# Hard-swish block's second product by Strassen, with its weights prepared on the chip and partly reloaded, and an earlier query transpose

## The chip, the cores and the metric

The kernel runs on one core of a Trainium2 chip. The metric is the device time of one execution in microseconds (us); the kernel before takes 975.52 us, the median of three runs (975.43 to 976.23). TensorE (PE) multiplies, ScalarE (ACT), VectorE (DVE) and GpSimd (POOL) work on elements, and SyncE (SP) issues the DMAs here. PEld is the loading of the stationary operand into TensorE, which overlaps the multiplying.

## The reference

Three stages follow each other. Chunked attention over 4 batches, 8 heads, 768 tokens of 64 (chunks of 32 with 16 keys to the left, 8 to the right, and 8 memory keys) gives x with 3072 tokens of 512. A first block of width 1024 with a gated softmax and a layer norm gives x2, again 3072 by 512. The third stage is the one that changes:

```python
def _moe2_ref(x, w_in, w_out):      # x: 3072 x 512, w_in: 512 x 2048, w_out: 2048 x 512
    h = x @ w_in
    relu6 = np.clip(h + 3.0, 0.0, 6.0)
    g = h * relu6 / 6.0
    return (g @ w_out).astype(np.float32)
```

Weights come as 64-bit floats, and the products are taken to float32 accuracy: each operand is split into a high and a low part of type fp32r, and a product is three matmuls, high by high, high by low and low by high.

## The kernel before

Tokens lie in 24 tiles of 128. A written-out list (FIRST) starts the pipeline, then a loop over tiles m = 7 to 23 runs the attention of the tiles ahead, the first product of block one for tile m (m1), its layer norm, and pieces of its second product (m2, called through piece) for groups of three tiles. Everything is issued in program order on each engine: there is no scheduler, so an engine's queue is the order of the calls, and a tile name (tag) that is used again makes the new writer wait for the last reader of the old content.

Inside a tile, block_p and block_e transpose the keys, p_p and p_e (line 467) the attention weights, v_p (line 476) multiplies them with the values, and q_p (line 410) transposes the queries of a later tile; v_p stands ahead of q_p. The third stage's weights are converted from 64 bits during the same loop (w2_abs, w2_hold, w2_bits), stored to DRAM as float32 (w2_store, w2d) and read back later (load_w2f, split_w2). The result x2 of block one goes through DRAM as well (m2_s, x2d, load_x2).

The third stage is a loop of 128 steps: 8 groups of 384 tokens by 16 slices of 128 of the inner width. In a step, g3 (line 649) makes 12 matmuls with a weight as the stationary operand and 384 token columns as the moving one. ACT and DVE then form the hard-swish r and split it into gh and gl. g4 (line 665) multiplies two steps later: for each of three token tiles, 3 matmuls with a 128 by 128 block of g stationary and 512 weight columns moving, 9 in all. Each matmul loads its stationary operand anew. All 32 weight slices lie split in SBUF from the first group on, so that in this stage only x2 is loaded and the output stored. The order of TensorE is g3 of step n, then g4 of step n-2:

```python
832         steps = [(gi, f) for gi in range(NG) for f in range(NF2)]
836                 g3(gi, f)
848                 g4(*steps[n - 2])
```

The functions that the diff touches, and what calls them:

## Time and profile before

| what | value |
|---|---|
| median of 3 runs | 975.52 us |
| the profiled execution | 976.84 us |
| its span in the profile | 975.1 us |
| PE busy | 947.0 us (97%) |
| weight loads (PEld) busy | 840.1 us (86%) |
| DVE / ACT / POOL busy | 53% / 42% / 16% |
| mean DMA rate over the span | 88 GB/s |
| granted TensorE clock | 0.997 of full speed |

A busy PE means that some matmul was in flight; since matmuls are pipelined, a row's duration is longer than the distance from one start to the next, and only that distance, or the time of a whole block of matmuls in the chain of waits, says what a matmul costs in a stream. Bounds between stages are read from the starts of the first and last matmul of a line.

### The profile page before, as it was taken

What the parts mean: (1) busy time and instruction counts of PE and PEld (TensorE: products, weight loads), DVE (VectorE), ACT (ScalarE), POOL (GpSimd) and SP (SyncE); (2) the same over time, 40 slices, a digit from 0 to 9 for tenths busy, and PEclk for the clock granted to TensorE, in tenths of its full rate; (3) what the DMA queues carried; (4) which work ended last, traced back from release to release, by engine and by line L of the source; (5) the groups of instructions that cost most, each with busy time, mean ns of one, the idle gap of its engine ahead of it and who ended that gap; (6) DMA issues with size and microseconds to landing.
All of it is one profiled execution on the core that took longest, in us unless ns stands there. A gap on an engine that the chain in (4) does not pass through costs nothing.

```text
span 975.1 us, 15592 instructions
## 1 busy us (share of the span) xinstructions
PE 947.0 (97%) x6108; PEld 840.1 (86%) x6108; DVE 517.7 (53%) x925; ACT 408.1 (42%) x730; POOL 154.6 (16%) x123
## 2 busy tenths in 40 slices
PE   5899899999999999999999999999999999999998
PEld 4677698888888888999999999999999999999997
DVE  6899977787878786446532232322322322323222
ACT  2568645656565654326432232332322322323322
POOL 3637742333332320000000000000000000000000
PEclk9999999999999999999999999999999999999999
DMA  9898156766766663144310010010010100100000
GB/s 179 162 215 193 53 146 192 170 165 188 180 174 179 166 163 93 66 132 134 118 41 25 1 66 1 1 65 1 1 65 1 59 6 1 66 1 1 33 1 32
DMA packets 129524, 86.16 MB, mean 88 GB/s; under 512 B 102828, under 2 KB 115116, under 8 KB 129452
## 3 DMA queue, kind: packets, MB, share of 16 engines
...
q8 instruction: 48, 0.79, 0.4%
...
## 4 chain that ended last, share of the span: by engine, by line
PE 77%; DVE 8%; issue 7%; DMA 4%; ACT 2%; POOL 1%; SPq 1%; DVEq 0%; POOLq 0%; ACTq 0%
PE ph L655 28%; PE acc L676 27%; PE m L599 9%; PE h L514 7%; PE tp L483 2%; PE sc L427 2%; DMA kn<-in_k_dram 1%; DVE lst L523 1%; PE tp L571 1%; DVE w2t L229 1%; DMA q_raw<-in_q_dram 1%; PE tp L414 1%; ACT pb L209 1%; DVE so L564 1%; DVE w2t L232 1%
## 5 line engine op out<-in xcount | busy, mean ns | idle before, releaser
L676 PE MATMUL acc<-w,gh 128*128 128x512 f32 x768 | 238.8, 392 | 0.0
L659 DVE SCALAR_TENSOR_TENSOR r<-r,ph 128x384 f32<-128x384 f32 x128 | 70.9, 554 | 278.4 <-ACT r L658 278.4
L658 ACT ACTIVATE r<-ph,three 128x384 f32<-128x384 f32 x128 | 74.4, 582 | 284.8 <-PE ph L655 284.8
L676 PEld LDWEIGHTS acc<-w,gh 128*128 128x128 f32 x768 | 142.3, 188 | 22.7
L676 PE MATMUL acc<-w,gl 128*128 128x512 f32 x384 | 151.1, 394 | 0.0
L655 PE MATMUL ph<-x,w 128*128 128x384 f32 x768 | 144.5, 336 | 0.0
L655 PE MATMUL ph<-x2h,w 128*128 128x384 f32 x512 | 141.0, 337 | 0.0
L655 PEld LDWEIGHTS ph<-x,w 128*128 128x128 f32 x768 | 136.0, 188 | 5.4
L237 DVE TENSOR_TENSOR gl<-r,gh 128x384 fp32r<-128x384 f32 x128 | 71.5, 558 | 75.7 <-ACT gh L236 75.7
L236 ACT ACTIVATE gh<-r 128x384 fp32r<-128x384 f32 x128 | 67.2, 525 | 80.0 <-DVE r L659 80.0
L655 PEld LDWEIGHTS ph<-x2h,w 128*128 128x128 f32 x512 | 93.7, 188 | 2.5
L599 PE MATMUL m<-lnh,wol 128*128 128x384 f32 x256 | 88.6, 346 | 1.5 <-POOL wol L327 0.9
L599 PE MATMUL m<-lnh,woh 128*128 128x384 f32 x256 | 88.2, 344 | 1.1 <-ACT woh L209 0.5
L599 PE MATMUL m<-lnl,woh 128*128 128x384 f32 x256 | 88.4, 345 | 0.3 <-DVE lnl L252 0.3
L655 PE MATMUL ph<-x2l,w 128*128 128x384 f32 x256 | 86.1, 336 | 0.0
L676 PEld LDWEIGHTS acc<-w,gl 128*128 128x128 f32 x384 | 72.0, 188 | 16.0
L514 PE MATMUL h<-w1h,xh 128*128 128x512 f32 x168 | 71.1, 423 | 0.0
L514 PE MATMUL h<-w1h,xl 128*128 128x512 f32 x168 | 67.1, 400 | 1.2 <-DVE xl L252 1.2
L514 PE MATMUL h<-w1l,xh 128*128 128x512 f32 x168 | 66.8, 398 | 0.0
L222 POOL TENSOR_SCALAR w2t<-w2t 128x512 f32<-128x512 f32 x32 | 63.0, 1983 | 8.7 <-ACT w2t L215 8.7
L248 ACT ACTIVATE lnh<-tp 128x512 fp32r<-128x512 f32 x41 | 24.3, 598 | 65.8 <-PE tp L571 65.8
L599 PEld LDWEIGHTS m<-lnh,wol 128*128 128x128 f32 x256 | 48.6, 190 | 2.4 <-POOL wol L327 1.2
...
## 6 DMA issues: line engine op xcount, KB each, us to landing
...
```

What stands on the lines that cost most here:

```text
L222: ENG[eng].tensor_scalar(out=tf, in0=tf, scalar1=U_LO, scalar2=U_HI, op0=ALU.max, op1=ALU.min)
L236: ACT.activation(out=hi, in_=r, func=AF.Copy)
L237: (eng or DVE).tensor_tensor(lo, r, hi.bitcast(F32), ALU.subtract)
L248: ACT.activation(out=hi, in_=r, func=AF.Copy)
L427: PE.matmul(sc[64 * x:64 * x + 64, c, s], qb[:, p, c].rearrange("k y t -> k (y t)"), kT[i % 2][:, p, c], start=True, stop=True)
L483: PE.matmul(po[64 * x:64 * x + 64, y, :, c * C:(c + 1) * C], vt[:, c, j], pb[:, c, j].rearrange("k s t -> k (s t)"), start=True, stop=True,)
L514: PE.matmul(h[:, f], a[:, kt], w[kt][:, f * 512:(f + 1) * 512], start=n == 0, stop=n == 3 * NKT - 1)
L599: PE.matmul(acc, w[fc // 2][:, fc % 2, dc * P:(dc + 1) * P], a[:, fc], start=n == 0, stop=n == len(todo) - 1)
L655: PE.matmul(ph, w[:, dc * P:(dc + 1) * P], xg[gi][a][:, dc], start=j == 0, stop=j == len(todo) - 1)
L658: ACT.activation(out=r, in_=ph, func=AF.Relu, bias=three, scale=1.0)
L659: DVE.scalar_tensor_tensor(out=r, in0=r, scalar=6.0, in1=ph, op0=ALU.min, op1=ALU.mult)
L676: PE.matmul(acc_t[t], a[:, sl], w, start=f == 0 and n == 0, stop=f == NF2 - 1 and n == 2)
```

## The change

The second product of the third stage, g @ w_out, is computed by Strassen's scheme: tokens are taken in 12 groups of 256 (two tiles) and the inner width in 8 pairs of slices, so that a step has a 2 by 2 grid of g blocks (128 by 128) and a 2 by 2 grid of weight blocks (128 by 256). Seven products of sums of blocks replace eight products of blocks. Of a step's 45 matmuls, all with 256 moving columns, 24 are of the first product and 21 (seven products, three each) of the second; there are 96 steps. POOL forms five sums of g blocks (one into q, four into s); ACT and DVE split two plain blocks with the sum in q, and then the four sums in s (split3). The seven products accumulate over the 8 pairs in four PSUM banks; at a group's end g_out copies three of them (ACT) and g_end combines them (six DVE operations, then two additions on POOL, or on DVE in the last group).

The five sums of weight blocks of each pair are formed by POOL during the tile loop (load_pair, sum_pair) and go to DRAM; prep splits them, and the two plain blocks, into seven high and low parts. SBUF holds six such sets at a time, and the pairs 1, 4 and 7 (USERS) share the tiles lh1 and km: their split sets are stored to DRAM once (store_prep) and read back by load_b, seven DMAs of 256 KB, each time after another user's products: 33 times in all. The weights of the first product (load_wi, split_wi) stay in SBUF. w1 of the first block moves to two larger tiles (wb0, wb1), which later hold prepared weights. In the tile loop the query transpose and its copies stand ahead of v_p for tiles of index 10 and above, and the last layer norm's transposes (ln_t) stand between the pieces of m2.

```diff
-    x2d = [dp.tile([P, NKT, G1], F32, name=f"x2d{i}") for i in range(NG)]
-    w2d = [dp.tile([P, 2, 512], F32, name=f"w2d{i}") for i in range(NF2)]
+    x2d = dp.tile([P, NKT, NT], F32, name="x2d")
+    w2d = [[dp.tile([P, 2, 512], F32, name=f"w2d{i}_{j}") for j in range(NF2 // 2)] for i in range(2)]
...
-        SP.dma_start(out=w2d[f][:, part], in_=raw["w2t", u].bitcast(F32))
+        SP.dma_start(out=w2d[part][f // 2][:, f % 2], in_=raw["w2t", u].bitcast(F32))
 
...
+    TG = 2 * P
+    NB = NT // TG
+    NS = NF2 // 2
+    USERS = (1, 4, 7)
+    B5_HOME = ("lh0", "lh1", "wb0", "wb1", "lh1", "ll1", "ll0", "lh1")
+    B2_HOME = (("kn0", "kn1"), ("km",), ("s0",), ("kT",), ("km",), ("q0", "q1"), ("s1",),
+               ("km",))
...
+    def load_pair(j):
+        raw["pair"] = T("xal", [P, 2, 2, 256], name="pair")
+        SP.dma_start(out=raw["pair"], in_=w2d[1][j].rearrange("p f (h c) -> p f h c", h=2))
+
+    def sum_pair(j):
+        w = raw["pair"]
+        t = raw["sums"] = T("x2r", [P, 5, 256], name="sums")
+        POOL.tensor_tensor(t[:, 0:2], w[:, :, 0], w[:, :, 1], ALU.add)
+        POOL.tensor_tensor(t[:, 2], w[:, 0, 0], w[:, 1, 1], ALU.add)
+        POOL.tensor_tensor(t[:, 3], w[:, 0, 1], w[:, 1, 1], ALU.subtract)
+        POOL.tensor_tensor(t[:, 4], w[:, 1, 0], w[:, 0, 0], ALU.subtract)
...
+    def prep():
+        j = PREPS[prep_n[1]]
+        prep_n[1] += 1
+        parts, d = raw["prep", j]
+        b5[j] = big(B5_HOME[j])[0]
...
+            split(t, b5[j][:, sl, 0], b5[j][:, sl, 1])
+        for k in range(2):
+            split(d[:, k], b2[j][k][:, 0], b2[j][k][:, 1])
+        load_prep()
+        store_prep()
+        to_store.append(j)
+
...
+    def load_b(j):
+        for u in (2, 3, 4, 1, 0):
+            SP.dma_start(out=b5[j][:, u].bitcast(F32), in_=b5_d[j][:, u])
+        for n in (1, 0):
+            SP.dma_start(out=b2[j][n].bitcast(F32), in_=b2_d[j][:, n])
...
-    def g3(gi, f):
-        n = gi * NF2 + f
-        ph = pp.tile([P, 512], F32, tag=("tp0", "tp1", "tp2", "sc")[n % 4], name="ph")[:, 0:G1]
-        wh, wl = w2h[f][:, 0], w2l[f][:, 0]
-        todo = [(dc, w, a) for dc in range(NKT) for w, a in ((wh, 0), (wh, 1), (wl, 0))]
-        for j, (dc, w, a) in enumerate(todo):
-            PE.matmul(ph, w[:, dc * P:(dc + 1) * P], xg[gi][a][:, dc],
-                      start=j == 0, stop=j == len(todo) - 1)
+    def g3(gi, j):
+        n = gi * NS + j
+        ph = pp.tile([P, 2, TG], F32, tag=("tp0", "tp1", "tp2", "sc")[n % 4], name="ph")
+        for k in range(2):
+            w = w2i[2 * j + k]
+            todo = [(dc, wl, xl) for dc in range(NKT) for wl, xl in ((0, 0), (0, 1), (1, 0))]
+            for m, (dc, wl, xl) in enumerate(todo):
+                PE.matmul(ph[:, k], w[:, wl, dc * P:(dc + 1) * P], xg[gi][xl][dc],
+                          start=m == 0, stop=m == len(todo) - 1)
+        ph_t[n] = ph.rearrange("p f t -> p (f t)")
...
+    def act3(gi, j):
+        n = gi * NS + j
+        rt = home(("pn", "pe")[n % 2], 896, F32)
+        r = rt[:, 0:512]
         ACT.activation(out=r, in_=ph, func=AF.Relu, bias=three, scale=1.0)
         DVE.scalar_tensor_tensor(out=r, in0=r, scalar=6.0, in1=ph, op0=ALU.min, op1=ALU.mult)
-        gh = T(("kn0", "kn1", "q0")[n % 3], [P, 512], F32R, name="gh")[:, 0:G1]
-        gl = T(("kT", "km", "q1")[n % 3], [P, 512], F32R, name="gl")[:, 0:G1]
-        split(r, gh, gl)
...
-            for n, (a, w) in enumerate(((gh, wh), (gh, wl), (gl, wh))):
-                PE.matmul(acc_t[t], a[:, sl], w, start=f == 0 and n == 0, stop=f == NF2 - 1 and n == 2)
...
+        POOL.tensor_tensor(q[:, 6], q[:, 0], q[:, 3], ALU.add)
+        POOL.tensor_tensor(s[:, 0:2], q[:, 0:2], q[:, 2:4], ALU.add)
+        POOL.tensor_tensor(s[:, 2:4], q[:, 1:3], q[:, 0:4:3], ALU.subtract)
...
+    def split3(gi, j, between=None):
+        n = gi * NS + j
...
+        split(q[:, 0:7:3], *ga)
+        if between is not None:
+            g_end(between)
+        tags = (("lh1", "ll1"), ("wb0", "wb1"))[n % 2]
+        gs = gS[n] = [extra(t).rearrange("p (b t) -> p b t", t=P) for t in tags]
+        split(s, *gs)
...
+    PRODUCTS = ((1, "A", 2, 5, 2), (3, "A", 0, 5, 3), (4, "A", 1, 5, 4), (5, "S", 0, 2, 1), (2, "S", 1, 2, 0),
+                (7, "S", 3, 5, 1), (6, "S", 2, 5, 0))
+    PLACE = {1: (0, 0), 3: (0, 1), 4: (1, 0), 5: (2, 0), 2: (2, 1), 7: (3, 0), 6: (3, 1)}
...
+    def g4(gi, j):
+        n = gi * NS + j
+        ga, gs = gA.pop(n), gS.pop(n)
+        for p, which, blk, wide, u in PRODUCTS:
+            a = ga if which == "A" else gs
+            w = b5[j][:, u] if wide == 5 else b2[j][u]
+            out = M(p)
+            for m, (al, wl) in enumerate(((0, 0), (0, 1), (1, 0))):
+                PE.matmul(out, a[al][:, blk], w[:, wl],
+                          start=j == 0 and m == 0 and PLACE[p][1] == 0, stop=j == NS - 1 and m == 2, skip_group_check=True)
...
+    def g_out(gi):
...
+        for t, n in ((e1, 1), (e3, 3), (e4, 4)):
+            ACT.activation(out=t, in_=M(n), func=AF.Copy, scale=1.0 / 6.0)
...
+    def g_end(gi):
...
+        for o, n, sign, t in ((c11, 5, -1, e1), (c22, 2, -1, e1), (c12, 5, 1, e3), (c21, 2, 1, e4),
+                              (c11, 7, 1, c11), (c22, 6, 1, c22)):
+            DVE.scalar_tensor_tensor(out=o, in0=M(n), scalar=sign / 6.0, in1=t, op0=ALU.mult, op1=ALU.add)
+        for o, t in ((c11, e4), (c22, e3)):
+            (DVE if gi == NB - 1 else POOL).tensor_tensor(o, o, t, ALU.add)
+        for t, o in enumerate((o1, o2)):
+            SP.dma_start(out=out[gi * TG + t * P:gi * TG + (t + 1) * P, :], in_=o)
...
                 s_norm(a, "P")
+            if m % 2 == 0:
+                sum_pair(m // 2 - 4)
...
             piece(m, 1)
+            if ok(n) and n >= BLOCKS:
+                q_p(n)
+                q_e(n, 0, "A")
+                q_e(n, 1, "A")
             if ok(a):
                 v_p(a)
...
+            if last:
+                split_x2(0, 0)
+                split_x2(0, 1)
+                load_wi(0)
+                load_wi(1)
...
-            if m == NTILE - 3:
+            if m % 2 == 0:
+                SP.dma_start(out=b5f[m // 2 - 4], in_=raw["sums"])
+            elif m < NTILE - 1:
+                load_pair(m // 2 - 3)
+            if m == NTILE - 2:
                 load_x2(0)
-                load_w2f(0)
-                load_w2f(1)
-            if m == NTILE - 1:
-                split_x2(0)
-                split_w2(0)
-                load_w2f(2)
+                load_prep()
+                load_prep()
         for j in range(4):
             piece(NTILE, j)
-        ln_t(NTILE - 1, 0)
-        ln_t(NTILE - 1, 1)
+            if j >= 2:
+                ln_t(NTILE - 1, j - 2)
+            if j in (0, 3):
+                prep()
...
+            if j in (1, 6):
+                prep()
...
-                        split_x2(gi + 1)
-            if n >= 2:
-                g4(*steps[n - 2])
+                    if j in (5, 6):
+                        split_x2(gi + 1, j - 5)
+            if n >= LAG:
+                gi, j = steps[n - LAG]
...
```

In the tile loop, on TensorE in the steady part, before: a piece of m2 (line 599), the product with the values (v_p, line 483), the query transpose (q_p, line 414), the next piece.

```order
L599 MATMUL m_2958<-lnh,woh 128x384
L599 MATMUL m_2958<-lnl,woh 128x384
L599 MATMUL m_2958<-lnh,wol 128x384
L483 MATMUL tp<-pb,v_96 64x2x32 x16
L414 MATMUL tp<-ident,q_raw 128x128 x4
L599 MATMUL m_3128<-lnh,woh 128x384
```

In the changed kernel the same place reads (the lines are 607, 491 and 422 there):

```order
L607 MATMUL m_4164<-lnh,woh 128x384
L607 MATMUL m_4164<-lnl,woh 128x384
L607 MATMUL m_4164<-lnh,wol 128x384
L422 MATMUL tp<-ident,q_raw 128x128 x4
L491 MATMUL tp<-pb,v_89 64x2x32 x16
L607 MATMUL m_4337<-lnh,woh 128x384
```

The four query transposes now stand between the piece and the product that needs pb.

On TensorE in the third stage, before, the end of a g3 block and a g4 block (w2 are the split weight slices, gh and gl the split hard-swish, acc the three token tiles' sums).

```order
L655 MATMUL ph_5365<-x2l_4712,w2_5248 128x384
L655 MATMUL ph_5365<-x2h_4711,w2_5249 128x384
L676 MATMUL acc_4998<-w2_5174,gh_5316 128x512
L676 MATMUL acc_4998<-w2_5175,gh_5316 128x512
L676 MATMUL acc_4998<-w2_5174,gl_5317 128x512
L676 MATMUL acc_5002<-w2_5174,gh_5316 128x512
L676 MATMUL acc_5002<-w2_5175,gh_5316 128x512
L676 MATMUL acc_5002<-w2_5174,gl_5317 128x512
L676 MATMUL acc_5006<-w2_5174,gh_5316 128x512
L676 MATMUL acc_5006<-w2_5175,gh_5316 128x512
L676 MATMUL acc_5006<-w2_5174,gl_5317 128x512
```

In the changed kernel, the end of a g3 block (line 762) and parts of the g4 block (line 816), of which an even step's rows stand here: b_xah and b_xal hold the plain g blocks and the sum in q, b_lh1 and b_ll1 the sums in s, b_wb0 and b_s0 prepared weights, b_wa9 a first-product weight, b_x2r and b_t1 the parts of x2.

```order
L762 MATMUL ph_5800<-b_t1_4693,b_wa9_5090 128x256
L762 MATMUL ph_5800<-b_x2r_4686,b_wa9_5090 128x256
L816 MATMUL acc_5207<-b_wb0_4809,b_xah_4765 128x256 x2
L816 MATMUL acc_5207<-b_wb0_4809,b_xal_4766 128x256
...
L816 MATMUL acc_5208<-b_s0_4810,b_lh1_5096 128x256 x2
L816 MATMUL acc_5208<-b_s0_4810,b_ll1_5109 128x256
...
L816 MATMUL acc_5209<-b_wb0_4809,b_lh1_5096 128x256 x2
L816 MATMUL acc_5209<-b_wb0_4809,b_ll1_5109 128x256
```

The blocks become 24 and 21 matmuls long, and every moving operand has 256 columns.

On SP's queue in the third stage, before: per group three output stores and one load of x2 (x2d_72 is one group's).

```order
L684 DMA out_dram<-o 128x512 x3
L635 DMA x2raw<-x2d_72 128x1536
L684 DMA out_dram<-o 128x512 x3
L635 DMA x2raw<-x2d_73 128x1536
L684 DMA out_dram<-o 128x512 x3
```

In the changed kernel, one group (b_lh and b_km are the shared tiles, b5d and b2d the stored sets):

```order
L742 DMA x2raw<-x2d 128x4x256
L736 DMA b_lh_5096<-b5d_94 128x512 x5
L738 DMA b_km<-b2d_97 128x512 x2
L736 DMA b_lh_5096<-b5d_95 128x512 x5
L738 DMA b_km<-b2d_98 128x512 x2
L736 DMA b_lh_5096<-b5d_93 128x512 x5
L738 DMA b_km<-b2d_96 128x512 x2
L838 DMA out_dram<-o 128x512 x2
```

Three reloads of seven DMAs each stand between a group's load of x2 and its output stores.

## Rows read from the trace of the kernel before

**Rows 1.** The page: busy time of the engines.

```profile
PE 947.0 (97%) x6108; PEld 840.1 (86%) x6108; DVE 517.7 (53%) x925; ACT 408.1 (42%) x730; POOL 154.6 (16%) x123
```

**Rows 2.** Busy time by stretch: PE, PEld, DVE, ACT, POOL, clock, DMA share, GB/s.

```profile
339.70:355.80 16.10, 15.86 (x141) 14.03 (x140) 12.99 (x24) 9.30 (x17) 5.38 (x5) 1.00 0.72 175
404.00:436.00 32.00, 31.47 (x180) 30.37 (x180) 16.23 (x28) 10.59 (x18) 0.55 (x1) 1.00 0.32 103
...
436.80:970.90 534.10, 534.07 (x2689) 484.50 (x2688) 175.42 (x303) 171.58 (x309) 0.00 (x0) 1.00 0.09 32
```

**Rows 3.** The chain that ended last, third stage: start us, us, what.

```profile
708.09 2.10 PE ph L655 x12
710.19 2.08 PE acc L676 x9
```

**Rows 4.** Groups by line: busy us, mean ns, idle before.

```profile
L658 ACT ACTIVATE r<-ph,three 128x384 f32<-128x384 f32 x128 | 74.4, 582 | 284.8 <-PE ph L655 284.8
L236 ACT ACTIVATE gh<-r 128x384 fp32r<-128x384 f32 x128 | 67.2, 525 | 80.0 <-DVE r L659 80.0
L236 ACT ACTIVATE w<-w2f 128x512 fp32r<-128x512 f32 x32 | 18.2, 618 | 7.5 <-DMA w2f<-w2d 7.5
...
L659 DVE SCALAR_TENSOR_TENSOR r<-r,ph 128x384 f32<-128x384 f32 x128 | 70.9, 554 | 278.4 <-ACT r L658 278.4
L237 DVE TENSOR_TENSOR gl<-r,gh 128x384 fp32r<-128x384 f32 x128 | 71.5, 558 | 75.7 <-ACT gh L236 75.7
L237 DVE TENSOR_TENSOR w<-w2f,w 128x512 fp32r<-128x512 f32 x32 | 20.6, 687 | 1.0 <-ACT w L236 1.0
...
L457 POOL TENSOR_TENSOR pn<-pe,ast 128x512 f32<-128x512 f32 x20 | 21.4, 1072 | 30.1 <-DVE ast L453 15.8 <-ACT e L529 7.3 <-ACT lnh L248 5.2
L252 POOL TENSOR_TENSOR lnl<-far,lnh 128x512 fp32r<-128x512 f32 x7 | 9.6, 1375 | 2.2 <-ACT lnh L248 2.0
```

**Rows 5.** Timeline of weight loads behind four transposes in the tile loop.

```profile
341.88 0.19 PEld L514 LDWEIGHTS h<-w1h,xh 128*128 128x128 f32 x1
341.99 0.19 PEld L514 LDWEIGHTS h<-w1l,xh 128*128 128x128 f32 x1
```

**Rows 6.** Timeline of TensorE at the same place.

```profile
341.91 0.48 PE L514 MATMUL h<-w1h,xh 128*128 128x512 f32 x1
342.23 0.40 PE L514 MATMUL h<-w1l,xh 128*128 128x512 f32 x1
```

**Rows 7.** Waits of TensorE, 200 to 420 us: total us, times, longest.

```profile
PE tp L483 <- ACT pb L209: 3.2, 11, 0.4
```

**Rows 8.** Timeline of a steady tile: the split of x, the next tile's first matmul, POOL.

```profile
351.15 0.69 DVE L252 TENSOR_TENSOR xl<-tp,xh 128x512 fp32r<-128x512 f32 x1
...
354.81 0.50 PE L514 MATMUL h<-w1h,xh 128*128 128x512 f32 x1
...
353.84 0.56 POOL L559 TENSOR_TENSOR lst<-lst,mhalf 128x1 f32<-128x1 f32 x1 [9.98 <-DVE lst L554]
```

**Rows 9.** Timeline of TensorE at the end of the tile loop.

```profile
419.44 0.44 PE L599 MATMUL m<-lnh,woh 128*128 128x384 f32 x1 [0.25 <-ACT lnh L248]
420.17 0.45 PE L599 MATMUL m<-lnl,woh 128*128 128x384 f32 x1 [0.28 <-DVE lnl L252]
```

**Rows 10.** Timeline of SP's queue at the end of a group.

```profile
641.60 1.53 SPq L684 DMA_DIRECT2D out_dram<-o  x3
643.18 0.44 SPq L635 DMA_DIRECT2D x2raw<-x2d  x1
```

**Rows 11.** Busy time in the stretch of those transfers.

```profile
642.40:647.40 5.00, 5.00 (x28) 4.61 (x27) 1.11 (x2) 1.11 (x2) 0.00 (x0) 1.00 0.87 315
```

**Rows 12.** Timeline of the end: last matmul, last copy.

```profile
970.48 0.39 PE L676 MATMUL acc<-w,gl 128*128 128x512 f32 x1
970.90 0.60 ACT L683 ACTIVATE o<-acc 128x512 f32<-128x512 f32 x1 [0.76 <-PE acc L676]
```

More of the change, by code (lines that the diff above doesn't have):

```diff
@@ L623, in load_w2f @@
[L623 to L638 removed]
+        SP.dma_start(out=x2d[:, dc, gi * G1:(gi + 1) * G1], in_=x2o[gi, dc])
@@ new lines, in sum_pair, with load_prep @@
+    def sum_pair(j):
[5 more added lines that the diff above has]
+        POOL.tensor_tensor(t[:, 4], w[:, 1, 0], w[:, 0, 0], ALU.subtract)
+    PREPS = (2, 3, 0, 6, 1, 5, 4, 7)
+    prep_n = [0, 0]
+    def load_prep():
+        n = prep_n[0]
+        prep_n[0] += 1
+        if n >= NS:
+            return
+        j = PREPS[n]
+        if n % 2 == 0:
+            t = home("x2r", 1536)[:, 0:1280].bitcast(F32).rearrange("p (u c) -> p u c", u=5)
+            parts = [(slice(0, 5), t)]
+        else:
+            parts = [(slice(0, 4), T("z1", [P, 4, 256], name="sums")), (slice(4, 5), T("e5", [P, 1, 256], name="sum"))]
+        d = home("xl", 512, F32) if n == NS - 1 else home(f"t{n % 2}", 512).bitcast(F32)
+        d = d.rearrange("p (k c) -> p k c", k=2)
+        for sl, t in parts:
+            SP.dma_start(out=t, in_=b5f[j][:, sl])
+        for k in range(2):
+            SP.dma_start(out=d[:, k], in_=w2d[1][j][:, k, 256 * k:256 * k + 256])
+        raw["prep", j] = parts, d
@@ L662, in g3 @@
[L662 to L684 removed]
+        q = rt.rearrange("p (b t) -> p b t", t=P)
@@ new lines, in tile_chunked_attention_solu_hardswish, with M @@
+    PRODUCTS = ((1, "A", 2, 5, 2), (3, "A", 0, 5, 3), (4, "A", 1, 5, 4), (5, "S", 0, 2, 1), (2, "S", 1, 2, 0),
+                (7, "S", 3, 5, 1), (6, "S", 2, 5, 0))
+    PLACE = {1: (0, 0), 3: (0, 1), 4: (1, 0), 5: (2, 0), 2: (2, 1), 7: (3, 0), 6: (3, 1)}
+    def M(n):
+        if not acc:
+            h = pp.tile([P, 2, 2, 256], F32, tag="h", name="acc")
+            acc[0], acc[1] = h[:, 0], h[:, 1]
+            for k in range(2):
+                acc[2 + k] = late[0].tile([P, 2, 256], F32, tag=f"m{k}", name="acc")
+        b, k = PLACE[n]
+        return acc[b][:, k]
@@ new lines, in tile_chunked_attention_solu_hardswish @@
+            if j in (2, 5, 8):
+                w = (j + 1) // 3
+                split_wi(w)
+                if w < 3:
+                    load_wi(w + 2)
+        load_wi(5)
+        steps = [(gi, j) for gi in range(NB) for j in range(NS)]
+        LAG = 2
+        for n in range(len(steps) + LAG):
+            if n < len(steps):
+                gi, j = steps[n]
+                g3(gi, j)
+                act3(gi, j)
+                if n in (0, 1, 3, 5):
+                    w = (4, 5, None, 6, None, 7)[n]
+                    split_wi(w)
+                    if w < 6:
+                        load_wi(w + 2)
+                if n in (0, 2, 4, 7):
+                    prep()
+                if n in (3, 6, 8):
+                    store_prep()
+                if gi + 1 < NB:
+                    if j == 3:
+                        load_x2(gi + 1)
+                    if j in (5, 6):
+                        split_x2(gi + 1, j - 5)
+            if n >= LAG:
+                gi, j = steps[n - LAG]
+                g4(gi, j)
+                if j in USERS and (gi > 0 or j == USERS[-1]):
+                    k = (USERS.index(j) + 1) % 3
+                    if not (gi == NB - 1 and k == 0):
+                        load_b(USERS[k])
+                if j == NS - 1:
+                    g_out(gi)
+            done = gi if n >= LAG and j == NS - 1 else None
+            if n < len(steps):
+                split3(*steps[n], done)
+            elif done is not None:
+                g_end(done)
```

154 lines of the change are left out of this document (81 added, 73 removed).

## The prediction

> **What bounds the kernel now.** I read the busy times first. TensorE has a matmul in flight for 97% of the span and no other engine passes 53% [rows 1]. The stretches show where that holds: in the third stage, from the first matmul of g3 at 436.8 us to the end of the last of g4 at 970.9, PE is busy 534.07 of 534.10 us at granted clock 1.00 (the 2.4 GHz level), DVE and ACT a third, POOL not at all, and the DMA engines 9% [rows 2]. The stage is TensorE's alone. The chain of waits prices it: a g3 block of 12 matmuls takes 2.10 us, a g4 block of 9 takes 2.08 [rows 3]. The tile loop is close to the same limit, 15.86 of 16.10 us in a tile [rows 2], with one regular hole ahead of v_p [rows 7].
>
> **What a matmul costs.** The stage's 534.1 us over 128 steps are 4.173 us a step. So a matmul of 384 columns costs 2.10 / 12 = 175.0 ns, and one of 512 costs (4.173 - 2.10) / 9 = 230.3 ns. No row has 256 columns. In proportion to columns (4.173 us / 9216) it would be 115.9 ns; along the straight line through both points (0.432 ns a column and 9.1 ns fixed) 119.7 ns. The nearest row is that of 384, where the fixed part weighs more than at 512, so I take 119, close to the line, and keep both ends.
>
> A new stationary operand is loaded for each matmul, and it must be ready within those 119 ns. The load's record lasts 0.19 us, which would forbid it, but behind four transposes of 128 columns the loads of two fp32r operands start 110 ns apart (341.88 and 341.99) [rows 5], and the second matmul starts 0.23 us after that, a normal distance for 512 columns [rows 6]. So the first load was in place 110 ns after its start; a load of 110 fits under 119.
>
> The Trainium skill (TensorE: Matmul & The Clock Gate, section Back-to-back issue gap) puts matmuls of N columns N/2.4 + 2.5 ns apart. By it 512 columns take 215.8 ns and 256 take 109.2; the trace shows 14.5 ns more at 512 [rows 3], and the measurement decides. The same page, section LDWEIGHTS, puts a load of 128 columns at 128/1.2 = 106.7 ns, and the trace agrees with 110 [rows 5].
>
> **The change, part by part.**
>
> Matmuls of the third stage. 128 x 12 of 384 and 128 x 9 of 512 columns go; 96 x 24 and 96 x 21 of 256 come. Columns of g3 stay the same, those of g4 fall by an eighth. 96 x 45 x 119 ns = 514.1 us against 534.1: **-20.0 us**. At 115.9 ns it is 500.7 (-33.4), at 119.7 it is 517.1 (-17.0). Break-even is 534.1 / 4320 = 123.6 ns.
>
> Element work in a step of now 45 x 119 = 5.36 us. ACT: the Relu on 512 columns (582 ns at 384, so up to 0.78), splits of 384 and 512 (0.525 + 0.618), 1.92 us. DVE: 0.74 + 0.56 + 0.69 = 1.99. POOL, new here: 640 columns at 1.07 to 1.38 us per 512, 1.3 to 1.7 us [rows 4]. In a row these make 0.78 + 0.74 + 1.7 + 0.62 + 0.69, about 4.6 us; from the end of g3(n) to the start of g4(n) stand two g4 and two g3 blocks, 90 matmuls or 10.7 us, and the two buffers of g sums come free with g4(n-2), 2.5 us after g3(n). Hidden: 0. If that cover went, PE would wait at g4 in each step.
>
> Reloads. 33 times SP issues seven DMAs of 262 KB, 1.835 MB. Each waits for the last reader of its slice, and behind it on SP stand only the next reloads, x2 and outputs. Before, 1.573 MB (three output stores, one load of x2) were issued from 641.60 on [rows 10], and the DMA engines worked at 315 GB/s up to 647.4 [rows 11]: 5.8 us with the latency, so 6.8 us for a reload. The tightest gap is from pair 7 to pair 1 of the next group. From the end of g4(7) to the fourth product of g4(1), the first to need a slice not released early, are two g3, one g4 and nine matmuls, 78 x 119 = 9.3 us; the other gaps have 5.4 us more. Hidden, 2.5 us to spare: 0. Bounds 0 to +3.
>
> Group ends. The accumulators are single, so the next group's first product waits for g_out and g_end. ACT has three copies of 256 columns (about 0.4 each), already released while g4 still runs, then a split (0.53); DVE a split (0.56) and six operations of about 0.4. Counted from the end of g4 the last ends near 3.1 us, while the first matmul that it releases starts after g3 and nine matmuls, 3.9 us. 0, bounds 0 to +3 for the 11 groups.
>
> Tile loop. The query transposes (0.43 us of PE work) now run while pb is copied: the 3.2 us of 11 waits go [rows 7]. Late next is the split of x, whose ACT half now follows two query copies (1.2 us); before, xl ended at 351.84 and the matmul that reads it came at 354.81 [rows 8]: 1.7 us remain. sum_pair adds 1280 columns on POOL, 2.7 to 3.4 us in every second tile; POOL works 5.4 of 16.1 us there [rows 2] and had been idle 9.98 us ahead of the one operation that the path needs [rows 8]. Its load and store add 1.2 MB per two tiles, 37 GB/s on 175 at 72% share [rows 2]. The waits of 0.25 and 0.28 us behind the last layer norm [rows 9] go with ln_t's new place. **-3.5 us**, bounds -3.7 to +1.
>
> Start of the third stage. Four prep calls (1792 columns each, about 2.1 us on ACT and 2.3 on DVE at the rates of the weight splits [rows 4]) come into a stretch where DVE works 16.2 and ACT 10.6 of 32 us [rows 2]. They fit, at 25 of 32 for DVE. In the first steps ACT and DVE have a weight split and a prep ahead of the first g split, and PE has only three g3 blocks (8.6 us) to cover it: **+1.5 us**, bounds 0 to +5.
>
> End. The last matmul ends at 970.87, the copy that its store needs at 971.50 [rows 12]. Now four combining operations run under the last products, but two more and two additions of about 0.4 us follow: **+1.5 us**, bounds +1 to +3.
>
> Sum: -20.0 - 3.5 + 1.5 + 1.5 = -20.5 us. The profiled execution took 976.84 us (span 975.1 and 1.7 around it), so 956.3; it was 1.3 us above the median of the runs, which makes 955.0 on the median's scale.
>
> **Rivals.**
>
> *The weight load sets the pace* (slower). At 512 columns a matmul takes 17.0 ns more than 512 / 2.4. If that is a hand-over that follows whichever of load and stream ends last, a matmul of 256 takes 110 + 17 = 127 ns, the stage 548.6 us, and the whole 990. For it: loads are busy 484.5 of 534.1 us already [rows 2], and would fill 92% of 119. Against: in the transposes loads repeat at 110 with the hand-over included [rows 5]. It decides from 123.6 ns on. 10%.
>
> *Reloads come late* (slower). At half the rate of rows 11 a reload takes 13.6 us, 4.3 more than the tightest gap; 11 times that is 47 us, and the whole 1002. For it: seven waits on one queue, 61 MB that were not moved before. Against: 5.8 us for 1.573 MB [rows 10, 11]. 5%.
>
> *Joints* (no change). Each g4 block now waits for several semaphores of ACT, DVE and DMA. At 0.2 us a block, a little under the short waits of rows 9, 96 blocks lose 19.2 us: about 974. Against: before, g4 waited on ACT and DVE too and lost nothing [rows 2]. 6%.
>
> *Matmuls at the weight load's pace of 110 ns* (much faster): 475.2 us for the stage, 916 in all. Against it stands the excess at 384 and 512. 4%. The gap rule of the Trainium skill cited above would give this, with the load as its floor.
>
> **How the numbers follow.** My case has 75%: the matmul at 115.9 to 119.7 ns with the bounds above, 939 to 973 when the ends go together. Within 0.2% (2 us, about what a measurement of this kernel can tell from no change) it holds 1%, slower another 1%. Faster: 0.73 + 0.04 + 0.02 (joints) = 0.79. Same: 0.01 + 0.03 = 0.04. Slower: 0.01 + 0.10 + 0.05 + 0.01 = 0.17. The range 938 to 976 holds my case and most of the joints, 0.80.
>
> **What would show it.** Right: a g3 block of 24 in 2.86 us and a g4 block of 21 in 2.50, PE without waits in the third stage, no wait of v_p on pb, reloads landed before the first product of their pair ends. Wrong: a distance of 123.6 ns or more between matmuls, waits of g4 on a DMA of the shared tiles, waits on ACT or DVE in most steps, or a first g4 that starts more than 5 us late.

## The result, and the profile after

The changed kernel takes 960.61 us, the median of four runs (960.15 to 960.85), beside 975.88 (975.43 to 976.26) for the kernel before: a ratio of 0.9843, interval 0.9826 to 0.9860. It is 15.3 us faster; 20.5 had been forecast. The page's busy times, of after; [rows 1] are those of before:

```profile
PE 924.3 (96%) x7740; PEld 867.3 (90%) x7740; DVE 604.1 (63%) x1043; ACT 450.2 (47%) x802; POOL 432.7 (45%) x465
```

PE has 1632 matmuls more and 22.7 us less to do; POOL's work has nearly trebled. Busy time by stretch, of after, with the columns of [rows 2]: two tiles of the tile loop that follow each other, and the third stage from its first matmul to the end of the last.

```profile
341.30:358.30 17.00, 16.02 (x145) 14.18 (x141) 14.02 (x26) 9.78 (x20) 6.48 (x6) 1.00 0.85 227
358.30:374.10 15.80, 15.80 (x142) 14.07 (x140) 13.09 (x24) 8.44 (x16) 8.37 (x8) 1.00 0.71 173
439.00:953.10 514.10, 512.06 (x4321) 511.44 (x4320) 245.15 (x403) 209.57 (x369) 246.31 (x310) 1.00 0.48 161
```

The third stage has gone from 534.1 to 514.1 us, the forecast for its matmuls alone (with the 1.5 us for its start it was 515.6), and loads now fill it. But one of the two tiles has PE idle for 1 us. Here is what each stretch of the profiled executions took (spans 975.1 and 958.6; the bounds are starts of matmuls, m1 being the first product of a tile):

| stretch | before | after | difference |
|---|---|---|---|
| start to m1 of tile 8 | 160.3 | 159.2 | -1.1 |
| m1 of tile 8 to m1 of tile 23 | 240.4 | 244.7 | +4.3 |
| m1 of tile 23 to the first g3 | 36.2 | 35.1 | -1.1 |
| third stage | 534.1 | 514.1 | -20.0 |
| end | 4.2 | 5.5 | +1.3 |

The first row is scatter: the kernel before with only the query move, below, has the same start and took 157.6 us for it. The -3.5 us forecast for the tile loop came out as +4.3. From m1 to m1, each tile takes:

| tile | 8 | 9 | 10 | 11 | 12 | 13 | 14 | 15 | 16 | 17 | 18 | 19 | 20 | 21 | 22 |
|---|---|---|---|---|---|---|---|---|---|---|---|---|---|---|---|
| before | 16.48 | 16.17 | 16.32 | 16.31 | 16.10 | 16.14 | 16.08 | 16.10 | 16.32 | 16.31 | 16.11 | 16.13 | 16.09 | 15.82 | 13.90 |
| after | 16.79 | 16.93 | 15.87 | 17.97 | 15.87 | 16.47 | 15.85 | 16.69 | 15.88 | 17.94 | 15.88 | 16.97 | 15.85 | 15.88 | 13.87 |

The even tiles from 10 to 20 won 0.2 to 0.45 us. The odd ones from 9 to 19 lost 0.3 to 1.7. What PE waited for between 150 and 440 us, in total, times and longest, of after ([rows 7] had the wait for pb before):

```profile
PE tp L491 <- ACT pb L209: 5.1, 6, 1.0
PE tp L407 <- DVE lnl L252: 1.5, 2, 0.8
```

The waits for pb are fewer but longer, and a new one has come. To follow it back, tiles 16 and 17: SP, POOL, DVE and PE, one row or two of each timeline of after (start us, us, engine, line, operation, idle time before it and what ended that).

```profile
292.85 2.18 SPq L180 DMA_DIRECT2D v<-in_mem_v_dram  x4
...
300.71 0.40 SPq L673 DMA_DIRECT2D pair<-w2d  x1
```

```profile
305.18 1.30 POOL L678 TENSOR_TENSOR sums<-pair 128x512 f32<-128x512 f32 x1 [8.28 <-DMA pair<-w2d]
...
308.50 0.57 POOL L567 TENSOR_TENSOR lst<-lst,mhalf 128x1 f32<-128x1 f32 x1
```

```profile
309.11 1.10 DVE L572 TENSOR_SCALAR so<-so,lst 128x1024 f32<-128x1024 f32 x1 [2.78 <-POOL lst L567]
```

```profile
316.79 0.66 PE L407 MATMUL tp<-ident,kn 128*128 128x128 f32 x4 [0.77 <-DVE lnl L252]
...
320.25 1.15 PE L491 MATMUL tp<-pb,v 128*64 128x64 f32 x32 [0.96 <-ACT pb L209]
```

SP issued the load of pair at the end of tile 15's instructions, behind the loads of v, and late (300.7): ahead of it stand eight loads more than usual, of the next batch's memory values (four from 292.85, four from 297.34). The same holds for the pair of tile 10, for which POOL waited 8.3 us too; the other five of its waits for a pair were of 2.9 to 5.1 us. sum_pair stands at the top of tile 16 in POOL's queue, so POOL stood 8.28 us with everything behind it. Behind it is the power of the layer norm (L567): DVE had its input ready at 306.3 and waited 2.78 us for it. DVE does not catch up: in tile 17 lnl and pb come late for PE. That is one idle POOL stretch of seven in the loop:

```profile
  DMA pair<-w2d: 34.0, 7
```

Behind tiles 8, 12, 14 and 18, where POOL waited only about 3 us, the odd tiles lost time in another way. There the sums ran beside the second of the tile's two conversions of raw weights on DVE. DVE in tile 18, of after, while POOL's sums ran from 333.87 to 338.32:

```profile
334.29 1.16 DVE L226 TENSOR_SCALAR w2t<-w2t 128x512 uint32<-128x512 uint32 x1
335.48 1.10 DVE L229 SCALAR_TENSOR_TENSOR w2t<-w2raw,w2t 128x512 uint32<-128x512 uint32 x1
336.62 1.10 DVE L232 SCALAR_TENSOR_TENSOR w2t<-w2raw,w2t 128x512 uint32<-128x512 uint32 x1
```

With no POOL work beside them these three take 0.42, 0.69 and 0.69 us. The conversion is 1.6 us longer, and in tile 19 PE waits 0.98 us for pb.

The third stage does what was forecast. A g3 block of 24 and a g4 block of 21 in the chain of waits, of after, which answer to [rows 3], and then all that PE waited for in the stage:

```profile
644.50 2.83 PE ph L762 x24
647.33 2.51 PE acc L816 x21
```

```profile
PE acc L816 <- DVE o L834: 1.3, 1, 1.3
PE acc L816 <- DVE b_xal L237: 0.8, 1, 0.8
```

The wait of 0.8 us is in the first g4 block; that of 1.3 ends at 493.6 us, where a product of the second group waits for g_end of the first. No wait is on a DMA. Groups by line in the stage, of after, which answer to [rows 4]:

```profile
L779 POOL TENSOR_TENSOR b_xh<-b_pn 128x256 f32<-128x256 f32 x48 | 52.6, 1096 | 0.0
L237 DVE TENSOR_TENSOR b_wb<-b_xh,b_wb 128x512 fp32r<-128x512 f32 x48 | 38.5, 802 | 45.6 <-ACT b_wb L236 45.6
L778 POOL TENSOR_TENSOR b_xh<-b_pe 128x256 f32<-128x256 f32 x48 | 37.7, 785 | 0.0
L773 ACT ACTIVATE b_pn<-ph,three 128x512 f32<-128x512 f32 x48 | 33.0, 687 | 39.7 <-PE ph L762 39.7
L777 POOL TENSOR_TENSOR b_pn<-b_pn 128x128 f32<-128x128 f32 x48 | 26.6, 555 | 131.1 <-DVE b_pn L774 130.2
```

POOL needs 1096 + 785 + 555 = 2.4 us a step, more than the 1.3 to 1.7 forecast, and still hides. The end: the last products, and the additions before the last store, answering to [rows 12].

```profile
952.22 0.88 PE L816 MATMUL acc<-b_lh,b_wb 128*128 128x256 f32 x6
...
954.48 0.75 DVE L836 TENSOR_TENSOR o<-o,b_xl 128x256 f32<-128x256 f32 x2
```

### The profile page after: what moved, and what is told of

Same layout as the page of the kernel before. It is cut to its first block, busy times and chain, and to the rows that moved or that the text cites. A ratio compares the mean times of both kernels' runs of the same rounds, so it can differ in the third digit from the quotient of the medians.

```text
span 958.6 us, 20195 instructions
## 1 busy us (share of the span) xinstructions
PE 924.3 (96%) x7740; PEld 867.3 (90%) x7740; DVE 604.1 (63%) x1043; ACT 450.2 (47%) x802; POOL 432.7 (45%) x465
## 4 chain that ended last, share of the span: by engine, by line
PE 71%; DVE 10%; DMA 7%; issue 4%; POOL 3%; SPq 3%; ACT 3%; DVEq 0%; ACTq 0%; POOLq 0%
PE ph L762 25%; PE acc L816 23%; PE m L607 9%; PE h L522 7%; DMA kn<-in_k_dram 3%; PE tp L491 2%; SPq L184 1%; PE sc L435 1%; DMA pair<-w2d 1%; PE tp L579 1%; DVE lst L531 1%; DMA v<-in_mem_v_dram 1%; DVE w2t L229 1%; DMA b5d<-b_lh 1%; ACT pb L209 1%
## 5 line engine op out<-in xcount | busy, mean ns | idle before, releaser
L522 PE MATMUL h<-w,xh 128*128 128x512 f32 x336 | 110.0, 409 | 0.0
L762 PE MATMUL ph<-b_x2r,b_wa 128*128 128x256 f32 x480 | 91.1, 281 | 0.0
L762 PE MATMUL ph<-b_xah,b_wa 128*128 128x256 f32 x480 | 90.7, 280 | 0.0
L762 PEld LDWEIGHTS ph<-b_xah,b_wa 128*128 128x128 f32 x480 | 76.1, 188 | 0.0
L762 PEld LDWEIGHTS ph<-b_x2r,b_wa 128*128 128x128 f32 x480 | 76.0, 188 | 0.0
L522 PEld LDWEIGHTS h<-w,xh 128*128 128x128 f32 x336 | 60.7, 191 | 11.7
L567 POOL TENSOR_TENSOR lst<-lst,mhalf 128x1 f32<-128x1 f32 x24 | 15.2, 634 | 124.2 <-DVE lst L562 124.2
L522 PE MATMUL h<-w,xl 128*128 128x512 f32 x168 | 67.0, 399 | 1.5 <-DVE xl L252 1.5
L762 PE MATMUL ph<-b_xal,b_wa 128*128 128x256 f32 x240 | 67.4, 281 | 0.0
L237 DVE TENSOR_TENSOR b_wb<-b_xh,b_wb 128x512 fp32r<-128x512 f32 x48 | 38.5, 802 | 45.6 <-ACT b_wb L236 45.6
L762 PE MATMUL ph<-b_t,b_wa 128*128 128x256 f32 x240 | 67.1, 280 | 0.0
```

Source lines behind the costliest of these rows:

```text
L237: (eng or DVE).tensor_tensor(lo, r, hi.bitcast(F32), ALU.subtract)
L522: PE.matmul(h[:, f], a[:, kt], w[kt][:, f * 512:(f + 1) * 512], start=n == 0, stop=n == 3 * NKT - 1)
L567: POOL.tensor_tensor(st[:, 10:11], st[:, 9:10], mhalf, ALU.pow)
L762: PE.matmul(ph[:, k], w[:, wl, dc * P:(dc + 1) * P], xg[gi][xl][dc], start=m == 0, stop=m == len(todo) - 1)
```

## Experiments

Times are medians; ratios are to the kernel before, run on the same chip (975.0 to 976.5 us there). The stretch is from m1 of tile 8 to m1 of tile 23: before 240.4, after 244.7. It is read from one execution each. The changed kernel's tile loop ran unaltered in four of the kernels here and took 244.7, 244.6, 244.5 and 243.5 us, so a difference of about 1 us between two stretches is not shown.

**The query move alone.** The kernel before, with only this:

```diff
+            if ok(n) and n >= BLOCKS:
+                q_p(n)
+                q_e(n, 0, "A")
+                q_e(n, 1, "A")
             if ok(a):
                 v_p(a)
...
-            if ok(n):
+            if n < BLOCKS:
                 q_p(n)
```

> The kernel before with the query transposes ahead of v_p, nothing else of the change. If the wait of v_p on pb is covered by the transposes: 975.9 less about 3 us, 972.8. Rival: a later engine takes the wait's place (the split of x behind two more ACT copies), 975.9.

972.84 us, 0.9968 (0.9956 to 0.9981), stretch 238.51; the wait of v_p for pb, against [rows 7], is now

```profile
PE tp L483 <- ACT pb L209: 0.2, 1, 0.2
```

The step is worth 2.9 us; it had been priced at 3.2. The stretch shows 1.9 of it, since tile 8 took 17.78 us in this execution (16.48 before).

**The query move undone** in the changed kernel:

```diff
-            if ok(n) and n >= BLOCKS:
-                q_p(n)
-                q_e(n, 0, "A")
-                q_e(n, 1, "A")
...
-            if n < BLOCKS:
+            if ok(n):
                 q_p(n)
```

> The changed kernel with the query transposes back behind v_p. If the move earns what the odd tiles show, 0.2 us a tile in 14 tiles, the whole goes from 960.6 to about 963.5. Rival: the even tiles' delays hide it, since there v_p waits for ACT anyway; then half of that, 962, or nothing.

961.77 us, 0.9854 (0.9841 to 0.9867), stretch 246.20. The move is worth 1.2 us there by the medians and 1.5 to 2.7 by the stretches, and the intervals of the ratios overlap, so its size is not shown. With the sums in the loop pb is late for other reasons too, and PE waits for it 8.2 us in 12 times.

**The sums left out.** Loads and stores keep their bytes; the store becomes two.

```diff
-        t = raw["sums"] = T("x2r", [P, 5, 256], name="sums")
-        POOL.tensor_tensor(t[:, 0:2], w[:, :, 0], w[:, :, 1], ALU.add)
...
+        raw["sums"] = w.rearrange("p f h c -> p (f h) c")
```

> The changed kernel without the five sums of weight blocks (left out: the stored sums are raw weight blocks); loads and stores of the same size stay. Theory A and rival B alike: even tiles become as short as odd ones, 15.9 us, the stretch from m1 of tile 8 to m1 of tile 23 is about 238.5 us, the whole about 954.5. Rival C (the added transfers): the stretch stays near 244 us, the whole at 960.

955.04 us, 0.9780 (0.9767 to 0.9793), stretch 239.63, ten tiles at 15.85 to 15.88. So the sums cost 5.1 us of the stretch (3.8 to 5.1 by the four executions of the changed loop) and 5.6 of the time; what else came into the loop, traffic included, costs about 239.63 - 238.51 = 1.1. In this order the step of +4.3 is -1.9 (queries) + 5.1 (sums) + 1.1.

**The pair loaded earlier**, at the top of the odd tile.

```diff
+            if m % 2 and m < NTILE - 1:
+                load_pair(m // 2 - 3)
...
-            elif m < NTILE - 1:
-                load_pair(m // 2 - 3)
```

> The changed kernel with load_pair issued at the top of each odd tile instead of its end, behind the value loads. Theory A (POOL's queue stands still behind sum_pair until the pair has landed, and the layer norm's power and the holds queue behind it): the pair lands before the next tile begins, the even tiles lose their 0.6 to 2.1 us, the stretch from m1 of tile 8 to m1 of tile 23 goes from 244.7 us to about 239, and the whole from 960.6 to about 955. Rival B (the sums on POOL slow DVE's operations beside them, whenever they run): the sums only move to other DVE work, 243 to 245 us and 959 to 961. Rival C (the added transfers make the raw weights late): unchanged, 960 to 961.

963.64 us, 0.9869 (0.9854 to 0.9884), stretch 247.88: slower than all three forecasts. POOL's wait for the pair went and the odd tiles fell to 15.88, but the even ones took 16.17 to 17.87, tile 18 18.35 and tile 12 20.96. There the raw weights that are due next came late behind the new load. ACT and then PE, of this kernel:

```profile
229.63 0.66 ACT L215 ACTIVATE w2t<-w2raw 128x512 f32<-128x512 f32 x1 [4.55 <-DMA w2raw<-in_moe_w_in_dram]
```

```profile
238.27 0.66 PE L407 MATMUL tp<-ident,kn 128*128 128x128 f32 x4 [2.16 <-DVE lnl L252]
```

**The pair loaded in the middle of the odd tile**, behind the issue of the raw weights:

```diff
                 end_w2(w2u[1])
+            if m % 2 and m < NTILE - 1:
+                load_pair(m // 2 - 3)
...
-            elif m < NTILE - 1:
-                load_pair(m // 2 - 3)
```

> The changed kernel with load_pair in the middle of each odd tile, behind the two loads of raw third-stage weights and ahead of the loads of q, k and v. Theory A (POOL's queue stands still behind sum_pair until the pair lands): the pair lands before the even tile begins, the odd tiles take 15.9 us as when it was loaded at the tile's top, and the raw weights are not delayed, so the even tiles stay under 16.6: the stretch from m1 of tile 8 to m1 of tile 23 is 240 to 242 us against 244.7, the whole 956 to 958. Rival B (what the sums do to the DVE work beside them costs as much as the wait): as with the load at the top, 246 to 248 us and 962 to 964.

958.82 us (957.86 to 962.83), 0.9844 (0.9821 to 0.9868), stretch 243.11. The odd tiles take 15.86 to 15.88, the even ones with the sums 16.38 to 16.52, and 8, 12 and 18 17.2 to 17.6. The result lies between the two theories: the wait for the pair explains 0.4 to 1.6 us of stretch, and a tile with sums still costs 0.5 or more.

**The sums behind w2_hold**, at the end of POOL's work in the even tile.

```diff
-            if m % 2 == 0:
-                sum_pair(m // 2 - 4)
...
                     w2_hold(u + 2, "P")
+            if m % 2 == 0:
+                sum_pair(m // 2 - 4)
```

> The changed kernel with sum_pair behind the tile's two holds on POOL instead of ahead of the layer norm's power; the load stays at the end of the odd tile. Theory A: nothing that the path needs stands behind the sums any more but the next s_norm, and DVE has no bit operations beside them; all tiles take 15.9 to 16.1 us, the stretch from m1 of tile 8 to m1 of tile 23 is about 239 us, the whole about 955, as without any sums. Rival B (the sums slow DVE whenever they run): 242 us or more, 958 or more.

961.01 us, 0.9861 (0.9846 to 0.9876), stretch 246.29: no gain, as rival B had it. Theory A failed in two ways. Another instruction of POOL that the path needs, the scaling of the attention weights (L465), now stands behind the sums. And DVE does have conversions beside them: in tiles 9, 13, 15 and 19 L229 and L232 took 1.10 to 1.11 us each. POOL, and PE's wait:

```profile
312.69 1.46 POOL L678 TENSOR_TENSOR sums<-pair 128x512 f32<-128x512 f32 x1
...
317.08 1.04 POOL L465 TENSOR_TENSOR pn<-pe,ast 128x512 f32<-128x512 f32 x1
```

```profile
PE tp L473 <- POOL pn L465: 5.1, 4, 2.7
```

**The sums two tiles after their load**, at the top of the next odd tile.

```diff
-            if m % 2 == 0:
-                sum_pair(m // 2 - 4)
+            jp = m // 2 - 4 if m % 2 and 9 <= m < NTILE - 1 else 7 if m == NTILE - 2 else None
+            if jp is not None:
+                sum_pair(jp)
```

> Nothing is left out: the pair is still loaded at the end of an odd tile, but the sums are formed two tiles later, at the top of the next odd tile behind POOL's s_norm, and stored at that tile's end, so that the pair has had a whole tile to land and the raw weights of the next tile are not pushed back. Theory A (the late pair that holds POOL's queue costs most of it): even tiles near 15.9 us, no wait of POOL for pair, odd tiles 15.9 to 16.4, the stretch from m1 of tile 8 to m1 of tile 23 about 242 and the time about 958. Theory B (the sums cost what they cost because they run beside VectorE's own element work, wherever they stand): odd tiles 16.5 or more, stretch 244 to 245, time within 1 us of the changed kernel's 960.6.

961.35 us (958.96 to 964.26), 0.9844 (0.9819 to 0.9868), stretch 247.76. The pattern of tiles is theory A's: even 15.85 to 15.88 from tile 10 on, the odd ones 9, 13, 15 and 19 16.26 to 16.47, POOL's wait for pair 0.3 us in all. The total is not, because of tiles 11 (21.09) and 17 (19.56), ahead of which SP issues eight DMAs more, for the next batch's memory values: there the raw weights come late. ACT in tile 11, of this kernel, and the windows behind it:

```profile
208.41 0.66 ACT L215 ACTIVATE w2t<-w2raw 128x512 f32<-128x512 f32 x1 [3.39 <-DMA w2raw<-in_moe_w_in_dram]
211.65 0.66 ACT L215 ACTIVATE w2t<-w2raw 128x512 f32<-128x512 f32 x1 [2.58 <-DMA w2raw<-in_moe_w_out_dram]
```

```profile
219.40:223.00 3.60, 3.60 (x32) 3.17 (x33) 3.46 (x10) 3.49 (x8) 0.26 (x1) 0.54 0.63 184
223.40:226.00 2.60, 2.60 (x19) 2.60 (x16) 1.61 (x5) 2.58 (x5) 0.07 (x1) 1.00 0.88 219
```

PE waited 1.08 and 2.16 us in tile 11, and behind that the granted clock was 0.54, near the 1.2 GHz level, for 3.6 us: a part of the tile's loss.

**The same, in two halves**: three of the four operations of sum_pair move behind w2_hold of the odd tile:

```diff
+    def sum_pair2(j):
+        w = raw["pair"]
+        t = raw["sums"]
         POOL.tensor_tensor(t[:, 2], w[:, 0, 0], w[:, 1, 1], ALU.add)
...
                     w2_hold(u + 2, "P")
+            if jp is not None:
+                sum_pair2(jp)
```

> As the run before it, but only the first 512 columns of the sums stand at the top of the odd tile; the other three sums of 256 stand behind w2_hold in the same tile. Theory A: no long hold of POOL in one place, so odd tiles stay under 16.3 us, the stretch is 241 to 242 and the time about 957. Theory B: the same work still runs beside VectorE's, so 244 to 245 and 960; s_norm of the next tile may queue behind the second half, which would show as a wait of PE for pn.

965.88 us, 0.9895 (0.9876 to 0.9914), stretch 249.51: both theories missed, and the halves are worse than the whole. Nine of the fifteen tiles take 16.6 to 16.9. POOL, DVE and PE in an odd tile, of this kernel:

```profile
282.88 1.73 POOL L678 TENSOR_TENSOR sums<-pair 128x512 f32<-128x512 f32 x1
```

```profile
283.50 1.66 DVE L232 SCALAR_TENSOR_TENSOR w2t<-w2raw,w2t 128x512 uint32<-128x512 uint32 x1
```

```profile
289.28 1.15 PE L491 MATMUL tp<-pb,v 128*64 128x64 f32 x32 [0.66 <-ACT pb L209]
```

One operation of POOL is enough for the whole loss of a tile, when it stands beside the bit operation L232 of DVE; the other three do the like in the next tile. So it is not the length of the sums that counts, but whose instruction they stand beside.

**The sums spread over tiles 9, 13, 14, 16, 19 to 22**, the pair loaded in the middle of the tile before, the sums stored right behind ln_pow.

```diff
+        SUM_AT = {9: 0, 13: 1, 14: 2, 16: 3, 19: 4, 20: 5, 21: 6, 22: 7}
...
-            if m % 2 == 0:
-                sum_pair(m // 2 - 4)
+            if m in SUM_AT:
+                sum_pair(SUM_AT[m])
...
                 end_w2(w2u[1])
+            if m + 1 in SUM_AT:
+                load_pair(SUM_AT[m + 1])
```

> Nothing is left out: the eight sums of pairs go to tiles 9, 13, 14, 16, 19, 20, 21 and 22, so that none stands in tiles 11, 12, 17 and 18, in or behind which SP issues the loads of a batch's beginning (eight DMAs more for the memory values); each pair is loaded in the middle of the tile before, and the sums are stored ahead of the loads at a tile's end. If what is left of the loss is a fixed 0.4 to 0.6 us for each tile whose sums run beside VectorE's work, plus the collisions with late raw weights in and behind tiles 11 and 17, then a tile with sums takes 16.3 to 16.5 us, the others 15.9, tiles 11 and 17 about 17 and 16.3 as without sums, the stretch is 242 and the time 957 to 958. If the collisions come wherever the sums stand, stretch 244 or more and 960.

957.59 us (955.81 to 958.59), 0.9812 (0.9797 to 0.9827), stretch 242.46. Tiles 9, 13, 14, 16, 19 and 20 take 16.47 to 16.60, 21 and 22 nothing more than without sums, tile 18 16.38, and the collisions at 11 and 17 are gone (16.63 and 15.87). Tile 14 with sums, and DVE's same operation in tile 15 without, of this kernel:

```profile
262.83 1.74 POOL L678 TENSOR_TENSOR sums<-pair 128x512 f32<-128x512 f32 x1
264.53 1.19 POOL L679 TENSOR_TENSOR sums<-pair 128x256 f32<-128x256 f32 x1
265.68 0.73 POOL L680 TENSOR_TENSOR sums<-pair 128x256 f32<-128x256 f32 x1
```

```profile
263.45 1.67 DVE L232 SCALAR_TENSOR_TENSOR w2t<-w2raw,w2t 128x512 uint32<-128x512 uint32 x1
...
280.06 0.69 DVE L232 SCALAR_TENSOR_TENSOR w2t<-w2raw,w2t 128x512 uint32<-128x512 uint32 x1
```

```profile
269.24 1.15 PE L491 MATMUL tp<-pb,v 128*64 128x64 f32 x32 [0.68 <-ACT pb L209]
```

How the one reaches the other stands in ACT's rows of tiles 14 and 15: its exponential waits for a reduction on DVE that stands behind L232, and the copy of pb stands behind the exponential.

```profile
266.89 1.12 ACT L537 ACTIVATE e<-h,lst 128x1024 f32<-128x1024 f32 x1 [1.79 <-DVE lst L531]
...
282.52 1.12 ACT L537 ACTIVATE e<-h,lst 128x1024 f32<-128x1024 f32 x1 [0.82 <-DVE lst L531]
```

L232 takes 0.98 us longer beside the sums, ACT waits 0.97 us longer, and PE waits 0.68 us for pb: the 0.7 us of the tile. Tiles 21 and 22 are the check on this. No raw weights are left to convert there, the sums take 1.29, 0.73, 0.74 and 0.74 us (the second row of tile 21 below), and the tiles are no longer than without sums (15.89 and 13.90 beside 15.88 and 13.90).

```profile
378.30 0.73 POOL L679 TENSOR_TENSOR sums<-pair 128x256 f32<-128x256 f32 x1
```

**The changed kernel again**, beside it on the same chip.

> The changed kernel once more, without any edit, beside the run before it on the same chip, for the difference between the two: 960.6 us as before, stretch 244.7 us. By the theory of fixed costs and collisions the spread version is 2 to 3 us below it, by the other it is the same.

958.70 us (957.37 to 962.39), 0.9835 (0.9814 to 0.9856), stretch 244.60. The spread version's stretch is 1.0 to 2.2 us below the four executions of the changed loop; in the time, the 1.1 us between the medians are within the spread of either. It is the fastest complete version here, not by a margin that is shown.

**The reloads left out**, so that the shared tiles keep one pair's weights:

```diff
-                        load_b(USERS[k])
+                        pass
```

> The changed kernel without the 33 reloads of shared weights (left out: from the second group on the pairs 1, 4 and 7 use whatever set lies in the shared tiles). If the reloads are hidden, as predicted: no change, 960 to 961, matmul distances of 118 and 119 ns as before. Rival: the traffic of 61 MB slows the matmuls or holds g4, then faster by more than 2 us.

959.96 us, 0.9849 (0.9834 to 0.9864). In the third stage the same two waits (1.2 and 0.8 us), the same blocks and the same 514.1 us. The reloads cost it nothing.

**A third of the matmuls of g3 cut to 128 columns**: the products with the low part of x2, 8 of 24 in a block.

```diff
-                PE.matmul(ph[:, k], w[:, wl, dc * P:(dc + 1) * P], xg[gi][xl][dc],
+                nc_ = P if xl else TG
+                PE.matmul(ph[:, k, 0:nc_], w[:, wl, dc * P:(dc + 1) * P], xg[gi][xl][dc][:, 0:nc_],
```

> The changed kernel with every third matmul of the first product cut from 256 to 128 moving columns (left out: the low part of x2 for half of the tokens); 768 matmuls. If the straight line through 384 and 512 goes on, one of 128 takes 64 ns and the whole falls by 41 us to about 920. If the weight load is a floor of about 110 ns, it falls by only 6 us to about 954.

956.62 us, 0.9808 (0.9791 to 0.9824), third stage 511.3: near the forecast of a floor, far from the straight line's. A block of 24 takes 2.793 us instead of 2.834. Half the columns of 8 matmuls at 2.4 GHz are 8 x 53 = 427 ns; 41 came back. PE, and the loads of two of the short matmuls, of this kernel:

```profile
640.24 0.45 PE L763 MATMUL ph<-b_xah,b_wa 128*128 128x256 f32 x2
640.52 0.22 PE L763 MATMUL ph<-b_xal,b_wa 128*128 128x128 f32 x1
640.58 0.45 PE L763 MATMUL ph<-b_xah,b_wa 128*128 128x256 f32 x2
640.87 0.22 PE L763 MATMUL ph<-b_xal,b_wa 128*128 128x128 f32 x1
```

```profile
640.06 0.19 PEld L763 LDWEIGHTS ph<-b_xal,b_wa 128*128 128x128 f32 x1
...
640.41 0.19 PEld L763 LDWEIGHTS ph<-b_xal,b_wa 128*128 128x128 f32 x1
```

The matmul behind a short one starts 0.06 us after it, so the matmuls could follow each other faster. Yet three take 0.35 us (640.52 to 640.87), 117 ns each: what a short one saves is lost again at the second matmul behind it. Three loads take 0.35 us as well (640.06 to 640.41). That is the pace of the loads. The Trainium skill (TensorE: Matmul & The Clock Gate, section LDWEIGHTS) gives a load of 128 columns 106.7 ns; in this stream a load and its matmul come every 2.793 / 24 = 116.4 ns, and the measurement decides. What the 10 ns between them are is open.

## Why the prediction was right, and where it was wrong

*The sum* (-20.5): the time fell by 15.3 us, and by 16.6 between the two profiled executions. That it came inside the range is owed to the third stage, and in part to luck: the tile loop missed its term by 7.8 us, and 1.1 us of that was made good by the scatter at the start.

*Matmuls of the third stage* (-20.0): right. g3 takes 2.834 / 24 = 118 ns a matmul, g4 2.504 / 21 = 119; PE is busy 512.06 us, 118.5 ns for each of the 4320. The matmuls alone gave -22.0, and the stage's -20.0 holds 2.1 us of waits. The reason was half right. "A load of 110 fits under 119" took one interval [rows 5] for the pace of a stream; where fewer columns go with the loads, they repeat at 116.4. So the loads were within 2 ns of setting the pace, and that a straight line through the columns gave nearly the same number (119.7) was in part luck. The rival of the weight load had the mechanism and the wrong price: no hand-over of 17 ns is added to a load, so 127 did not come. Joints did not cost either: PE waited in no g4 block but two.

*Element work, reloads, group ends* (0): right but for 1.3 us at the first of the 11 group ends, within the bounds; the waits after and the run without reloads show it. POOL's 2.4 us a step in place of 1.3 to 1.7 was mis-sized, but the cover of 10.7 us was ample.

*Start of the third stage and its end* (+1.5, +1.5): 0.8 us of waits at the first g4, and +1.3. The stretch ahead of the stage was 1.1 us shorter for all its four prep calls (a call's DVE time at the rate of rows 4 is 2.4 us, not 2.3, which changes nothing).

*Tile loop* (-3.5, bounds -3.7 to +1): wrong, at +4.3. The first half of the step held: the query move alone is worth 2.9 us. The half that failed is "sum_pair adds 1280 columns on POOL, 2.7 to 3.4 us in every second tile; POOL works 5.4 of 16.1 us there [rows 2] and had been idle 9.98 us ahead of the one operation that the path needs [rows 8]". The length was about right (1.30 + 0.74 + 0.74 + 0.75 = 3.5 us in tile 16), the idle time was there, and the cost was 5.1 us for all that. Two things were left out. POOL takes its instructions in order, and the first of the sums waited up to 8.3 us for a load that SP issued last in the tile before, so that the idle time lay ahead of sum_pair and the layer norm's power behind it. And DVE, though it works only 12.99 of 16.10 us [rows 2], has no slack where it counts, because its operations stand in a row ahead of pb. Beside the sums L226, L229 and L232 took 1.16, 1.10 and 1.10 us in place of 0.42, 0.69 and 0.69 in the changed kernel, and L232 took 1.67 in the versions with the pair loaded in time; such a tile costs PE 0.2 to 1.0 us.

Against the kernel without sums, tiles 11 and 17, behind the two waits of 8.3 us, are 0.9 and 1.7 us longer, and tiles 9, 13, 15 and 19, behind tiles with sums beside the conversion, 0.6 to 1.1 each; tiles 8 and 18 are 1.0 shorter together. So both causes are shown, and neither size is exact: the version with the pairs loaded in time and away from a batch's start won 1.0 to 2.2 us of the stretch, and the rest of what the sums cost is put down to DVE. The run without the sums took 955.04; the forecast for the whole was 955.0, so the sums are as large as the whole miss. One reading of the prediction was off without effect: the matmul at 354.81 [rows 8] reads xh, and xl is read two matmuls later, so more than 1.7 us remained there.

The Trainium skill states the second (SBUF — State Buffer, section SBUF: two separate sides): a VectorE operation with two inputs in SBUF and a GpSimd operation that reads SBUF hold one pair of ports by turns, each for its whole length. The rows of tile 14 with the spread sums agree: L232 starts at 263.45, the sum before it ends at 264.57, and 0.69 us later would be 265.26 (it ended at 265.12); the next sum, 0.73 us by itself, takes 1.19 and ends at 265.72. DVE's subtraction L252, with one input in PSUM, takes 0.68 us beside the sums and without them. The prediction had not weighed it, though the trace of before has it: there L229 takes 0.69 us alone, and this beside POOL's scaling of the attention weights (342.82 to 343.86):

```profile
342.98 1.43 DVE L229 SCALAR_TENSOR_TENSOR w2t<-w2raw,w2t 128x512 uint32<-128x512 uint32 x1
```

What stays open: which part of the 1.1 us of "what else" is traffic, and how the 5.1 us divide exactly between the late pair and DVE.
